# The middle of a decode block's feed-forward as four rows of 448, and w2 with 14 adjacent rows per partition

## Chip, cores, metric

One core of one Trainium2 chip. The metric is the device time of one launch in microseconds. The times are those of repeated runs; the profile is one run of each kernel. All runs told here are in the state that the measurement calls fast.

## The reference

A transformer block for one token: a conditioning vector gives six shifts, scales and gates; grouped-query attention over a cache of 32768 keys; then a feed-forward of width 1792. The part that matters here is the second half:

```python
def _B_ref(x, w1, w2):                       # x [1,1,512], w1 [512,1792], w2 [1792,512]
    h = jnp.einsum('bsd,df->bsf', x, w1)
    h = jnp.maximum(h, jnp.zeros_like(h))
    return jnp.einsum('bsf,fd->bsd', h, w2)
...
h = _layernorm(x, axis=-1) * (1 + cb) + sb
x = x + gb * _B_ref(h, B_w1, B_w2)
```

All weights and the cache are bfloat16. Nearly all of the 149 MB that are read is the cache; w1 and w2 (1.84 MB each) are read last.

## The kernel before

The whole input goes through one DMA queue, in the order in which it is needed: K and V per head group, then wo in four pieces, w1 in two (contraction rows 0 to 2, then row 3 of each partition), w2 in six. The feed-forward before:

```python
FB = 2; FA = FT // FB                                    # FT = 14, FA = 7
w2_v = B_w2.rearrange("(a p b) d -> p a b d", p=P, b=FB) # 2 adjacent rows of w2 per partition and block of 256
W2P = [(0, 2, slice(0, FB)), (2, FA - 5, slice(0, FB)), (FA - 3, 1, slice(0, FB)), (FA - 2, 1, slice(0, FB)),
       (FA - 1, 1, slice(0, 1)), (FA - 1, 1, slice(1, FB))]
...                                                      # second layernorm gives h2T [128, 4], as columns
for part, (k0, k1) in enumerate(W1P):                    # hidden row straight as columns: 4 x 14 matmuls of 1 column
    w1_f = need(("w1", part)).rearrange("p kt (a m b) -> p kt a b m", m=P, b=FB)
    for kt in range(k0, k1):
        for ft in range(FT):
            nc.tensor.matmul(hidT_ps[:, ft:ft + 1], lhsT=w1_f[:, kt - k0, ft // FB, ft % FB, :],
                             rhs=h2T[:, kt:kt + 1], start=False, stop=(kt == KT - 1), ...)
        if kt < KT - 2:
            keep_clock(1)                                # a matmul that nobody reads
nc.scalar.activation(out=<diagonals of hid_bd>, in_=hidT_ps[:].unsqueeze(2).to_broadcast([P, FT, KT]), func=ACT.Relu)
keep_clock(1)
for part, (base, n, bs) in enumerate(W2P):               # 14 x 4 matmuls, output 4 rows of 128
    w2_sb = need(("w2", part))
    ...
                nc.tensor.matmul(ffn_ps, lhsT=hid_bd[:, ft, i, :], rhs=w2_sb[:, a, b - bs.start, i * P:(i + 1) * P], ...)
nc.vector.tensor_tensor(out=o_rows[:], in0=ffn_ps, in1=gb_rows[:], op=ALU.mult)   # the two last VectorE
nc.vector.tensor_tensor(out=o_bf[:], in0=o_rows[:], in1=x1_rows[:], op=ALU.add)   # instructions, then the store
```

## Time and profile before

| | before |
|---|---|
| time, median of the first 3 runs | 355.95 us (355.69 to 356.25) |
| span of the profiled run | 353.6 us |
| HBM read | 149.42 MB, 423 GB/s over the span |
| second layernorm's result h2T starts | 344.52 us |
| last two VectorE instructions start | 350.88 us |

A line of the timeline begins with start and duration in us, then engine, source line, operation, output and input tile, and in brackets how long the engine had stood idle and what ended that. PE is TensorE, PEld its weight loads, DVE VectorE, ACT ScalarE. The lines of this kernel stand in the prediction.

### The profile page before, as it was taken

The numbers are of one execution on the slowest core, as the hardware profiler recorded it, in microseconds if no ns is written. First come the engines' busy times: TensorE is split into PE (matmuls) and PEld (weight loads), VectorE is DVE, ScalarE is ACT, GpSimd is POOL, SyncE is SP. The second block draws the span as 40 slices with busy tenths as digits, with TensorE's granted clock in tenths as the row PEclk, the third lists the DMA queues.
The fourth block names the chain that finished last, engine by engine and source line by source line (L and its number), as shares of the span: only waits on it lengthen the run. The fifth ranks groups of instructions, "written<-read, shape, count | busy, mean of one in ns | idle before, by whom it ended". The sixth has DMA issues, their size and how long they took to land. (4 is left out here: it accounts for less than half of the span.)

```text
span 353.6 us, 4077 instructions
## 1 busy us (share of the span) xinstructions
PE 281.0 (79%) x1351; PEld 113.2 (32%) x1351; DVE 208.0 (59%) x269; ACT 28.2 (8%) x68; POOL 9.7 (3%) x16
## 2 busy tenths in 40 slices
PE   0273781899798979897979796989789787989996
PEld 0031230333243323332433233333333233334445
DVE  7737684982858367572949177553938095743040
ACT  1023004000110011001100101010100010020000
POOL 8200000000000000000000000000000000000000
PEclk9986997699899999998999998799999999999999
DMA  8999999999999999999999999999999999999995
GB/s 309 459 419 430 454 412 423 449 434 419 439 445 419 437 449 417 423 452 426 419 439 445 419 437 442 426 425 445 434 415 441 441 424 423 452 426 413 426 417 197
DMA packets 7108, 149.59 MB, mean 423 GB/s; under 512 B 824, under 2 KB 1080, under 8 KB 2232
## 3 DMA queue, kind: packets, MB, share of 16 engines
q1 hardware_dynamic: 7032, 149.43, 98.5%
q8 instruction: 8, 0.13, 0.1%
q14 instruction: 4, 0.03, 0.0%
q0 software_dynamic: 64, 0.00, 0.0%
HBM read 149.42 MB, written 0.00 MB: 423 GB/s over the span
## 5 line engine op out<-in xcount | busy, mean ns | idle before, releaser
L411 DVE STREAM_TRANSPOSE KTt<-Ksb 128x2048 f32<-128x2048 f32 x64 | 143.3, 2284 | 64.1 <-DMA Ksb<-in_A_k_cache_dram 55.8
L493 PE MATMUL o_ps<-Vsb,PT_g 128*16 (+1 forms) x512 | 129.6, 391 | 21.6 <-ACT qbd L395 9.6
L431 PE MATMUL S_ps<-KTt,qbd 128*128 128x512 bf16 x512 | 122.3, 390 | 18.6 <-DVE KTt L411 17.2
L431 PEld LDWEIGHTS <-qbd 128*128 128x128 bf16 x512 | 49.0, 98 | 83.1 <-issue 25.4
L493 PEld LDWEIGHTS o_ps<-Vsb,PT_g 128*16 x416 | 37.0, 89 | 90.3 <-issue 64.3
L437 DVE TENSOR_SCALAR_CACHE_REDUCE S_g<-S_ps 128x512 f32<-128x512 f32 x16 | 11.0, 690 | 27.6 <-PE S_ps L431 27.6
L395 ACT COPY qbd<-qrep_sb 32x128 bf16<-32x128 bf16 x32 | 9.4, 295 | 135.6 <-PE S_ps L431 134.5
L474 DVE STREAM_TRANSPOSE PT_g<-P_g 128x1024 bf16<-128x1024 bf16 x8 | 9.7, 1218 | 6.6 <-ACT P_g L468 6.6
L465 ACT ACTIVATE nbias<-Mb_ps 128x1 f32<-128x1 f32 x8 | 1.4, 171 | 132.0 <-PE Mb_ps L463 132.0
L233 PE MATMUL xc_ps<-cx_sel,cx_bd 16*128 16x2 bf16 x4 | 0.3, 171 | 14.5 <-DVE cx_bd L227 14.5
L493 PEld LDWEIGHTS <-PT_g 128*16 128x16 bf16 x96 | 8.2, 90 | 11.0
L468 ACT ACTIVATE P_g<-S_g,nbias 128x1024 bf16<-128x1024 f32 x8 | 9.2, 1148 | 0.2
L179 DVE COPY sel<-ident_bf 128x128 bf16<-128x128 bf16 x4 | 8.1, 3936 | 1.1 <-POOL ident_bf masks.py:199 1.1
L524 DVE SCALAR_TENSOR_TENSOR Y<-o_ps,smask,Y 16x128 f32<-16x128 f32 x24 | 8.1, 338 | 0.8
L480 PE MATMUL L_ps<-Lexp,ones_f 128*128 128x4 f32 x16 | 3.0, 257 | 4.3 <-DVE Lexp L477 4.3
L606 PE MATMUL spare_ps<-qbd,ident_bf 128*128 128x512 bf16 x19 | 5.9, 380 | 0.0
L452 DVE TENSOR_REDUCE Mrow<-mT_ps 1x4 f32<-1x128 f32 x8 | 2.1, 257 | 5.9 <-PE mT_ps L449 5.9
L449 PE MATMUL mT_ps<-ident_f,m_p 128*1 128x128 f32 x8 | 2.2, 270 | 3.9 <-DVE m_p L446 2.0
L480 PEld LDWEIGHTS L_ps<-Lexp,ones_f 128*128 128x128 f32 x16 | 3.1, 221 | 5.8 <-issue 5.1
L233 PEld LDWEIGHTS <-cx_bd 16*128 16x128 bf16 x4 | 0.2, 113 | 14.5 <-DVE cx_bd L227 14.5
L543 DVE TENSOR_TENSOR oT_sb<-acc_ps,Linv 128x4 bf16<-128x4 f32 x8 | 1.2, 151 | 5.7 <-PE acc_ps L530 5.7
L368 PE MATMUL q_ps<-wq_sb,hT 128*1 128x512 bf16 x32 | 3.5, 621 | 1.2 <-DVE hT L284 1.2
(114 smaller groups left out, 89.1 us busy)
## 6 DMA issues: line engine op xcount, KB each, us to landing
Ksb<-in_A_k_cache_dram SPq DMA_DIRECT2D x16, 4096.0 KB, 28.2
Vsb<-in_A_v_cache_dram SPq DMA_DIRECT2D x15, 4096.0 KB, 24.6
wq_sb<-in_A_wq_dram SPq DMA_DIRECT2D x1, 4096.0 KB, 19.5
Vsb<-in_A_v_cache_dram SPq DMA_DIRECT2D x2, 2048.0 KB, 23.3
wm_sb<-in_w_mod_dram SPq DMA_DIRECT2D x1, 3072.0 KB, 10.3
wo_sb<-in_A_wo_dram SPq DMA_DIRECT2D x1, 2048.0 KB, 25.0
w_sb<-in_B_w_dram SPq DMA_DIRECT2D x1, 1344.0 KB
wo_sb<-in_A_wo_dram SPq DMA_DIRECT2D x1, 1024.0 KB, 27.1
```

Source lines behind the costliest of these rows:

```text
L179: nc.vector.tensor_copy(out=sel[:, hp, :].rearrange("p (a c) -> p a c", a=4), in_=src)
L368: nc.tensor.matmul(q_ps[i][32 * a:32 * a + 1, :].rearrange("o (h e) -> o h e", e=32), lhsT=hT[:, kt:kt + 1], rhs=wq_f[:, kt, i, a], start= ...
L395: nc.scalar.copy(out=o, in_=i)
L411: t = nc.vector.transpose(out=KTt[:].bitcast(F32), in_=Ksb[:, 32 * half:32 * half + 32, :].rearrange("p j d -> p (j d)").bitcast(F32),)
L431: nc.tensor.matmul(S_ps_tiles[g], lhsT=qbd[g % 2][:, hp, s, :], rhs=KTv[:, 16 * sl:16 * sl + 16, h, :, par], start=(t4 == 0 and sl == 0 an ...
L437: nc.vector.tensor_scalar(out=S_tiles[g][:, G, :], in0=S_ps_tiles[g], scalar1=1.0, scalar2=None, op0=ALU.mult, op1=ALU.max, accum_out=m_ti ...
L468: nc.scalar.activation(out=P_g[:], in_=S_g[:].rearrange("p g f -> p (g f)"), func=ACT.Exp, bias=nbias[:], scale=scale, accum_out=l_g[:],)
L474: nc.vector.transpose(out=PT_g[:], in_=P_g[:])
L480: nc.tensor.matmul(L_ps[:], lhsT=ones_f[:], rhs=Lexp[:], start=True, stop=True)
L493: nc.tensor.matmul(o_tiles[g][:], lhsT=PT, rhs=Vx, start=False, stop=False, skip_group_check=True)
L524: nc.vector.scalar_tensor_tensor(out=Y[:], in0=o[:, s], scalar=smask[:, s:s + 1], in1=Y[:], op0=ALU.mult, op1=ALU.add,)
L606: nc.tensor.matmul(spare[0], lhsT=ident_bf[:], rhs=qbd[0][:, 0, 0:4, :], start=True, stop=True)
```

## The change

Its intent is a shorter way from the second layernorm to w2, and longer runs of memory for w2. The hidden row is computed as rows: h2T is the stationary operand and 448 columns of w1 move past it, four such quarters side by side in the array. VectorE's transpose of 32x32 blocks turns them to columns. Row 448q + 14e + f of the hidden layer then stands at partition 32q + e, so that partition must hold 14 adjacent rows of w2.

```diff
-    W2P = [(0, 2, slice(0, FB)), (2, FA - 5, slice(0, FB)), ...]
+    W2P = [(0, 4), (4, 8), (8, 10), (10, 12), (12, 13), (13, 14)]
-    w2_v = B_w2.rearrange("(a p b) d -> p a b d", p=P, b=FB)
+    w2_v = B_w2.rearrange("(p f) d -> p f d", p=P)
@@ in the attention's tail @@
+        hid_ps = ps_o.tile([P, 512], F32, tag="o", name="hid_ps")
+        nc.vector.memset(hid_ps[:], 0.0)
@@ feed-forward @@
-                for ft in range(FT):
-                    nc.tensor.matmul(hidT_ps[:, ft:ft + 1], lhsT=w1_f[...], rhs=h2T[:, kt:kt + 1], ...)
-                if kt < KT - 2:
-                    keep_clock(1)
+                for q in range(4):
+                    nc.tensor.matmul(hid_ps[32 * q:32 * q + 1, 0:NQ], lhsT=h2T[:, kt:kt + 1],
+                                     rhs=w1_sb[:, kt - k0, q * NQ:(q + 1) * NQ], ...)
+        keep_clock(4)
+        hidT = rows_sb("hidT")...
+        nc.vector.transpose(out=hidT, in_=hid_ps[:, 0:NQ].rearrange("p (e f) -> p f e", f=FT))
         nc.scalar.activation(
-            in_=hidT_ps[:].unsqueeze(2).to_broadcast([P, FT, KT]), func=ACT.Relu,
+            in_=hidT[:, :, 0:1].to_broadcast([P, FT, KT]), func=ACT.Relu,
         )
-        keep_clock(1)
```

(cut; the six pieces keep their sizes, 512, 512, 256, 256, 128 and 128 KB, and the 56 matmuls with w2 stay)

More of the change, by code (lines that the diff above doesn't have):

```diff
@@ L50 @@
     LOOPED = Hkv - 2
-    FB = 2
-    FA = FT // FB
-    W2P = [(0, 2, slice(0, FB)), (2, FA - 5, slice(0, FB)), (FA - 3, 1, slice(0, FB)), (FA - 2, 1, slice(0, FB)),
-           (FA - 1, 1, slice(0, 1)), (FA - 1, 1, slice(1, FB))]
+    W2P = [(0, 4), (4, 8), (8, 10), (10, 12), (12, 13), (13, 14)]
     W1P = [(0, KT - 1), (KT - 1, KT)]
-    assert Dh == 128 and REP == 4 and D == 512 and Dff % (FB * P) == 0 and NTILE == 4
+    assert Dh == 128 and REP == 4 and D == 512 and FT == W2P[-1][1] and NTILE == 4
     scale = float(Dh) ** -0.5
@@ L125, in load @@
         else:
-            a0, n, bs = W2P[key[1]]
-            nb = bs.stop - bs.start
-            t = piece("w12_sb", KT * Dff + (a0 * FB + bs.start) * D, n * nb * D)
-            t = t.rearrange("p (a b d) -> p a b d", a=n, b=nb)
-            src = w2_v[:, a0:a0 + n, bs]
+            f0, f1 = W2P[key[1]]
+            t = piece("w12_sb", KT * Dff + f0 * D, (f1 - f0) * D).rearrange("p (f d) -> p f d", d=D)
+            src = w2_v[:, f0:f1]
         stream_dma(t[:], src)
@@ L693 @@
         project(3)
-        hidT_ps = small_ps([P, FT], "hidT_ps")
-        nc.vector.memset(hidT_ps[:], 0.0)
         stat2 = const.tile([P, 2], F32)
@@ L716 @@
         nc.vector.tensor_copy(out=x1_rows[:], in_=x1_ps[0])
+        NQ = 32 * FT
         for part, (k0, k1) in enumerate(W1P):
-            w1_f = need(("w1", part)).rearrange("p kt (a m b) -> p kt a b m", m=P, b=FB)
+            w1_sb = need(("w1", part))
             for kt in range(k0, k1):
-                for ft in range(FT):
+                for q in range(4):
                     nc.tensor.matmul(
-                        hidT_ps[:, ft:ft + 1], lhsT=w1_f[:, kt - k0, ft // FB, ft % FB, :], rhs=h2T[:, kt:kt + 1],
-                        start=False, stop=(kt == KT - 1), skip_group_check=True,
-                    )
-                if kt < KT - 2:
-                    keep_clock(1)
+                        hid_ps[32 * q:32 * q + 1, 0:NQ], lhsT=h2T[:, kt:kt + 1],
+                        rhs=w1_sb[:, kt - k0, q * NQ:(q + 1) * NQ], start=False, stop=(kt == KT - 1),
+                        skip_group_check=True,
+                    )
+        keep_clock(4)
+        hidT = rows_sb("hidT").rearrange("p a b -> p (a b)")[:, 0:NQ].rearrange("p (f e) -> p f e", e=32)
+        nc.vector.transpose(out=hidT, in_=hid_ps[:, 0:NQ].rearrange("p (e f) -> p f e", f=FT))
         hb = hid_bd[:]
@@ L729 @@
             out=AP(hb.tensor, hb.offset, [hb.ap[0], [KT * KT, FT], [KT + 1, KT]]),
-            in_=hidT_ps[:].unsqueeze(2).to_broadcast([P, FT, KT]), func=ACT.Relu,
+            in_=hidT[:, :, 0:1].to_broadcast([P, FT, KT]), func=ACT.Relu,
         )
-        keep_clock(1)
         ffn_ps = bank("ffn_ps")[0:KT, 0:P]
-        last = len(W2P) - 1
-        for part, (base, n, bs) in enumerate(W2P):
+        for part, (f0, f1) in enumerate(W2P):
             w2_sb = need(("w2", part))
-            for a in range(n):
-                for b in range(bs.start, bs.stop):
-                    ft = (base + a) * FB + b
-                    for i in range(KT):
-                        nc.tensor.matmul(
-                            ffn_ps, lhsT=hid_bd[:, ft, i, :], rhs=w2_sb[:, a, b - bs.start, i * P:(i + 1) * P],
-                            start=(part == 0 and a == 0 and b == 0 and i == 0), stop=(ft == FT - 1 and i == KT - 1),
-                        )
+            for ft in range(f0, f1):
+                for i in range(KT):
+                    nc.tensor.matmul(
+                        ffn_ps, lhsT=hid_bd[:, ft, i, :], rhs=w2_sb[:, ft - f0, i * P:(i + 1) * P],
+                        start=(ft == 0 and i == 0), stop=(ft == FT - 1 and i == KT - 1),
+                    )
         o_rows = const.tile([KT, P], F32)
```

## The prediction

> **What bounds the kernel now.** I read four views in this order: the page (bytes, chain of work that ended last), the timeline of the last ten microseconds, the DMA queue's own timeline in slices (for the landings), and the instructions of the few lines that the change resembles.
>
> The page first.
>
> ```profile
> span 353.6 us, 4077 instructions
> PE 281.0 (79%) x1351; PEld 113.2 (32%) x1351; DVE 208.0 (59%) x269; ACT 28.2 (8%) x68; POOL 9.7 (3%) x16
> DMA  8999999999999999999999999999999999999995
> HBM read 149.42 MB, written 0.00 MB: 423 GB/s over the span
> DMA Vsb<-in_A_v_cache_dram 7%; DMA w_sb<-in_B_w_dram 5%; PE ffn_ps L742 1%; SPq L139 0%; DVE o_rows L747 0%; DVE o_bf L749 0%
> ```
>
> The row of DMA digits is at 9 from the second slice to the last but one: 149 MB are streamed once, and no engine is as full. The chain ends in two transfers, 40 matmuls and two small VectorE instructions. The change does not touch one byte of the total, so it can only act in the tail, behind the last weight transfers. The chain in order of time gives the tail:
>
> ```profile
> 331.74 16.67 DMA w_sb<-in_B_w_dram
> 348.45 2.41 PE ffn_ps L742 x40
> 350.88 0.29 DVE o_rows L747
> 351.19 0.28 DVE o_bf L749
> ```
>
> The piece of w2 that was issued at 331.74 landed at about 348.41. It is the second of six, and the 40 matmuls after it are those of pieces 2 to 6 (10 rows per partition, 4 matmuls each). The timeline shows what lies ahead of them:
>
> ```profile
> 344.52 0.22 DVE L284 SCALAR_TENSOR_TENSOR h2T<-cen_ln,rstd_ln,modT_sb 128x4 bf16<-128x4 f32 x1
> 344.77 0.42 PEld L721 LDWEIGHTS <-w_sb 128*128 128x128 bf16 x14 [0.46 <-DMA w_sb<-in_B_w_dram]
> 345.93 0.84 PE L721 MATMUL hidT_ps<-h2T,w_sb 128*128 128x1 bf16 x28
> 346.86 0.29 ACT L728 ACTIVATE hid_bd<-hidT_ps 128x56 bf16<-128x56 f32 x1 [2.58 <-PE hidT_ps L721]
> 347.24 1.05 PE L742 MATMUL ffn_ps<-w_sb,hid_bd 128*4 128x128 bf16 x16 [0.23 <-ACT hid_bd L728]
> 348.45 2.39 PE L742 MATMUL ffn_ps<-w_sb,hid_bd 128*4 128x128 bf16 x40 [0.16 <-DMA w_sb<-in_B_w_dram]
> ```
>
> Read the brackets: the last line waits for a DMA, not for the hidden row. The 16 matmuls of piece 1 end at 347.24 + 1.05 = 348.29 and then TensorE has nothing until 348.45.
>
> Landings, as issue plus time to landing of each transfer (from the DMA view in narrow windows): w1 rows 0 to 2 at 344.75 (where the issuing engine's wait for that transfer also ends), w1 row 3 at 322.42 + 23.4 = 345.82; w2 pieces 1 to 6 at 326.86 + 20.2 = 347.06, 331.74 + 16.7 = 348.42, 336.59 + 12.5 = 349.09, 339.03 + 10.7 = 349.73, 340.28 + 9.7 = 349.98 and 341.55 + 8.8 = 350.35. So the whole tail runs at the pace at which bytes arrive. The 40 matmuls are 39 gaps of (2.39 - 0.219)/39 = 0.0557 us and a last one of 0.219 us. Without any wait all 56 from 347.24 would end at 347.24 + 55 x 0.0557 + 0.219 = 350.52, against 350.84 in the trace: 0.32 us of slack on the side that computes the hidden row. And the last piece, landing at 350.35, needs 4 matmuls, 3 x 0.0557 + 0.219 = 0.39: 350.74 at the earliest. Two floors made of transfers, 350.84 and 350.74, lie close together.
>
> **What the Trainium skill says.** "TensorE: Matmul & The Clock Gate", section "Part 3: Packing small matmuls — row/col tiling": outputs at PSUM partitions 0, 32, 64 and 96 sit in separate column groups of the array, and their matmuls run together. The trace agrees: the 16 matmuls of one output row and 512 columns for the attention projection took 1.08 us, 67 ns each, where one alone shows 378 ns. "VectorE: DVE Perf Modes", section "The three transpose paths": VectorE transposes 32x32 blocks only. That is why each quarter of the hidden row is put at a partition that is a multiple of 32, and why partition 32q+e must then own 14 adjacent rows of w2. "DMA: Bandwidth & Descriptors", section "Why small descriptors are slow (HBM only)": a fixed overhead of about 3 cycles per packet, named for 256-byte ones. The trace leans the same way at larger sizes: 432 GB/s from 20 to 320 us with a mean packet of 29 KB, 400 and 388 GB/s in 345.82 to 347.06 and 347.06 to 348.44, with DMA share at 1.04 and 1.03. "TensorEngine Tiling (Array Packing)", section "Tiling Modes": changing the mode drains the array. No line isolates that cost; the mode is changed twice here, where TensorE waits anyway.
>
> **The change part by part.**
>
> Removed: 56 one-column matmuls for the hidden row (rows 0 to 2 with two clock-keeping matmuls between, 344.80 to about 346.3, row 3 to 346.77) and the 0.07 us memset of their 14 columns.
>
> Added on TensorE: 16 matmuls of one row by 448 columns. A round of four took, in the like group, (1.08 - 0.378)/15 x 4 = 0.187 us at 512 columns; I take 0.19 for 448. Rows 0 to 2 start at 344.80 as now and are through their issue at 344.80 + 3 x 0.19 = 345.37. Then row 3 of w1 isn't there: it lands at 345.82. Here the old order was never kept waiting, since it got to row 3 only at about 346.3; the new one is. From 345.85 the last round takes 3 x 0.047 + 0.35 (one matmul, 0.378 less the shorter row) = 0.49 at most; the four overlap nearly wholly, so 0.36 to 0.49, and I take 0.40: 346.25.
>
> Added on VectorE: the transpose of 128x448 float32 out of PSUM, read with a stride. The like instruction, 128x512 with a stride of 4, took 0.705 us, the contiguous one 0.696: the stride costs nearly nothing. Less 64 elements at 0.97 per ns (the long transposes: 2048 in 2284 ns, 512 in about 700, so 1536 in 1584 ns), 0.066: 0.64 us. Start 0.04 after the matmuls (the gap between 350.84 and 350.88): 346.29 to 346.93.
>
> Moved on ScalarE: the relu now reads SBUF with a stride of 32. It took 294 ns on 56 columns; the cast of 16 columns from a strided SBUF tile took 216. I keep 0.28: 346.97 to 347.25. First matmul of w2 at about 347.33, against 347.24. The path through the hidden row is therefore no shorter: 0.52 us gained at the end of the matmuls (346.77 to 346.25), 0.64 + 0.04 paid for the transpose, a little back on the relu; about 0.1 us later. That fits in the slack of 0.32: 56 matmuls from 347.33 end at 350.61.
>
> Four clock-keeping matmuls, 0.213 us apart, begin after the 16 and end by about 347.1, before the relu: nothing.
>
> The new memset of 128x512 takes 0.485 us of VectorE at about 333.5, where VectorE is idle for over 3 us: nothing. The order of instructions, compared engine by engine, is otherwise unchanged, and the issues of the eight weight transfers have the same sizes and waits.
>
> Transfers: pieces 1 and 2 of w2, 512 KB each, become runs of 4 KB instead of 2 KB; pieces 3 and 4 stay at 2 KB, 5 and 6 at 1 KB. Row 3 of w1 is already made of 3.5 KB runs at the pitch that w2 gets (14336 bytes): 448 KB between 344.75 and 345.82, 429 GB/s between the landings, against 1048576 B in 2.60 us = 403 GB/s for the two pieces. At 429 they take 2.44: up to 0.16 us earlier for everything behind. The windows put less difference on it (381 GB/s in row 3's stretch), so I take 0.08.
>
> Sum: piece 2 lands at 348.34, end of matmuls 348.34 + 0.03 + 2.39 = 350.76; last piece at 350.27, 350.27 + 0.03 + 0.39 = 350.69; hidden-row path 350.61. The latest counts: 350.76 against 350.84, so 0.08 us earlier; the two VectorE instructions and the store stay. 355.95 - 0.08 = 355.87 us.
>
> **The rivals.**
>
> 1. The transpose path becomes the bound. It would need the relu to end over 0.25 us later than I have it: a strided PSUM read at half speed adds 0.47 us to the transpose and 0.2 to 0.3 us to the time, 356.2. The like transpose with stride 4 speaks against it; a stride of 14 has no line here.
> 2. The transfers gain the full 0.16 us or more and the hidden path stays in its slack: 355.75. For it, the 429 GB/s; against it, the last two 1 KB pieces, where the rate falls to 221 GB/s and less whatever comes before.
> 3. The scattered runs (4 KB out of every 14 KB, instead of a solid 256 KB block) cost the transfers 5%: 2.60 us becomes 2.73, 356.05. Row 3 of w1, with the same pitch, speaks against it.
> 4. TensorE drops its clock in the wait from 345.37 to 345.82. The granted clock is 1.00 in all of the last 24 us, and the gap is too short beside gaps already there (0.23). At half speed 56 matmuls would take 3 us more, 358 us. Unlikely.
>
> **Range and chances.** All but the last rival lie within 0.3 us. The three runs of before span 0.56 us (355.69 to 356.25), more than any of it, and the profiled run was 355.37; so the range is set by the scatter: 355.3 to 356.4. Two per cent are 7.1 us, and the whole stretch from the second layernorm to the end is 9.0 us (342.49 to 351.47), so most of it would have to vanish: faster 0.01, within 2% 0.98, slower 0.01.
>
> **What would show it right or wrong.** In the new trace: 12 matmuls of 448 columns, then a wait of about 0.4 us that a weight transfer ends; a transpose of 0.64 us; a relu of under 0.3 us ending at about 347.25; the 40 last matmuls still ahead of a DMA wait, or no wait at all before the first 20; landings of pieces 2 and 6 0 to 0.16 us earlier. A transpose over 0.9 us or a granted clock below 1 would speak for rivals 1 or 4; later landings at equal rates up to 345 us for rival 3. A difference that arises before 344 us would mean that something I hold untouched was moved.

## The result, and the profile after

The changed kernel took 355.41 us, median of 6 runs (355.13 to 355.82); the kernel before took 355.82 us in its 6 runs (355.47 to 356.27). A ratio is the mean time of one kernel's fast runs over that of the other's fast runs of the same rounds, so not quite the ratio of the medians: 0.9988, with a 95% interval of 0.9975 to 1.0001. That is "same" at two per cent, and the interval just touches 1.

The timeline of the changed kernel, from the layernorm's result to the last VectorE pair:

```profile
344.33 0.22 DVE L278 SCALAR_TENSOR_TENSOR h2T<-cen_ln,rstd_ln,modT_sb 128x4 bf16<-128x4 f32 x1
344.67 0.74 PE L717 MATMUL hid_ps<-w_sb,h2T 128*1 128x448 bf16 x12
345.66 0.36 PE L717 MATMUL hid_ps<-w_sb,h2T 128*1 128x448 bf16 x4 [0.25 <-DMA w_sb<-in_B_w_dram]
346.07 0.65 DVE L724 STREAM_TRANSPOSE hidT<-hid_ps 128x448 f32<-128x448 f32 x1 [1.32 <-PE hid_ps L717]
346.82 0.33 ACT L726 ACTIVATE hid_bd<-hidT 128x56 bf16<-128x56 f32 x1 [2.71 <-DVE hidT L724]
347.19 3.37 PE L736 MATMUL ffn_ps<-w_sb,hid_bd 128*4 128x128 bf16 x56 [0.20 <-ACT hid_bd L726]
350.61 0.28 DVE L741 TENSOR_TENSOR o_rows<-ffn_ps,gb_rows 4x128 f32<-4x128 f32 x1 [3.88 <-PE ffn_ps L736]
```

Twelve matmuls run, then TensorE waits for row 3 of w1, as foretold. The whole tail here lies 0.19 us earlier than in the profile of before already at h2T. This is the prediction's own sign that something untouched was moved ("a difference that arises before 344 us"), but it comes from the stream of transfers, which varies from run to run: its last packet of 32 KB ended at 321.46 us here and at 321.66 before, ahead of the first changed instruction (the memset at 333.50), and in the other profiles below at 321.5 to 322.1. From the start of h2T to the start of the last VectorE pair it is 350.61 - 344.33 = 6.28 us, against 350.88 - 344.52 = 6.36 before: 0.08 us less, the number predicted.

The 56 matmuls stand in one line because no idle time shows between them, but 3.37 us is 0.09 more than the 55 x 0.0557 + 0.219 = 3.28 that they need without a wait. A matmul shows 0.219 us and the next starts 0.056 after it, so a wait of under 0.16 us can't be seen as idle time. The landing of piece 2 (the end of its transfer, as its semaphore tells) says where it is: issued at 331.56, landed at 348.13, while matmul 17 was ready at 347.19 + 16 x 0.0557 = 348.08. With the 0.04 us from landing to first matmul that the kernel before shows (348.41 to 348.45) this is the 0.09. So both floors, the hidden row and piece 2, now lie within 0.1 us of each other.

The packets changed as the diff says. Times below are computed from the packets of the two traces (medians; the size is the run of memory):

```
bytes    before: count, ns    after: count, ns    bytes per ns
 4096          256   159           512   159         25.8
 2048          768    84           256    84         24.4
 1024          256    46           256    46         22.3
32768         4096  1213          4096  1213         27.0
```

A packet costs some 9 ns and 1 ns per 27.2 bytes. Pieces 1 and 2 are 256 packets fewer, 16 per transfer engine, so 16 x 9 = 0.14 us of transfer by this estimate. Piece 2 landed at 348.41 before (331.74 + 16.67; the prediction's "331.74 + 16.7 = 348.42" doesn't add up, but its result is only 0.01 off) and at 348.13 after: 0.28 us earlier, less some 0.2 of the whole stream.

The traces hold the landings to the nanosecond, and with row 3 of w1 as the mark the stream's own scatter drops out. From the landing of row 3 to that of piece 2, the five profiles with w2 as before (before, e1, e1b, e7, e7b) have 2.57 to 2.63 us; the eight with the new layout (changed kernel twice, e2, e4, e8, e8b, e9, e11) have 2.51 to 2.56. The means are 2.616 and 2.537: the longer runs bring piece 2 forward by 0.08 us, about half of the estimate.

### The profile page after: what moved, and what is told of

Read it like the earlier page. It is cut to its first block, busy times and chain, and to the rows that moved or that the text cites. A ratio compares the mean times of both kernels' runs of the same rounds, so it can differ in the third digit from the quotient of the medians.

```text
span 353.3 us, 3999 instructions
## 1 busy us (share of the span) xinstructions
PE 282.0 (80%) x1310; PEld 112.9 (32%) x1312; DVE 209.1 (59%) x270; ACT 28.3 (8%) x68; POOL 9.7 (3%) x16
## 5 line engine op out<-in xcount | busy, mean ns | idle before, releaser
L425 PE MATMUL S_ps<-KTt,qbd 128*128 128x512 bf16 x512 | 124.6, 396 | 17.0 <-DVE KTt L405 15.6
L295 PE MATMUL mod_ps<-wm_sb,siluT 128*1 128x512 bf16 x24 | 3.6, 624 | 1.1 <-DVE siluT L289 1.1
```

Of the source, the lines that this page charges most:

```text
L295: nc.tensor.matmul(dst[j // 4][32 * (j % 4):32 * (j % 4) + 1, :], lhsT=src_T[:, kt:kt + 1], rhs=w[:, kt, j * 512:(j + 1) * 512], start=(kt ...
L425: nc.tensor.matmul(S_ps_tiles[g], lhsT=qbd[g % 2][:, hp, s, :], rhs=KTv[:, 16 * sl:16 * sl + 16, h, :, par], start=(t4 == 0 and sl == 0 an ...
```

## The experiments

Theory A, that of the prediction: landings set the end, the longer runs of w2 bring piece 2 forward, and the hidden row's path stays in its slack. Rival B: the new way from h2T to the relu brings the gain. Rival C: the transfers have room, the runs' size is indifferent. Theory D came after the first four runs and is told there. The edits are shown shortened.

### Four rows and transpose alone, w2 as before: e1_rows_only, e1b_rows_only

```diff
+    W2P, w2_v, load and the last 56 matmuls as in the kernel before
-                        rhs=w1_sb[:, kt - k0, q * NQ:(q + 1) * NQ], ...
+                        rhs=w1_sb[:, kt - k0, :].rearrange("p (a q x) -> p a q x", q=4, x=64)[:, :, q, :], ...
-        nc.vector.transpose(out=hidT, in_=hid_ps[:, 0:NQ].rearrange("p (e f) -> p f e", f=FT))
+        nc.vector.transpose(out=hidT.rearrange("p (a b) e -> p a b e", b=FB),
+                            in_=hid_ps[:, 0:NQ].rearrange("p (a e b) -> p a b e", a=FA, b=FB))
```

> The four rows and the transpose alone, with w2 as before (pieces of 2 adjacent rows per partition, runs of 2 KB). Theory A (the end is set by landings, the new runs of 4 KB bring piece 2 some 0.1 us forward, the hidden row stays inside its slack): piece 2 lands as in the kernel before, TensorE waits for it, and from the end of the second layernorm (h2T) to the first of the two last VectorE instructions it takes 6.36 us as before, not 6.28 as in the changed kernel; the time is that of before within 0.2 us. Rival B (the faster matmuls of the hidden row bring the gain): 6.28 us, as in the changed kernel, and no wait before matmul 17 of the last 56.

The first version gave a wrong result (relative error 0.053): I had put the axes of the transpose's input in the order a, e, b. Its times are still of use, since the same instructions run on other values, but for the order in which the transpose reads: 355.35 us median of 5 runs (before, in those rounds, 355.96). The profile: h2T at 344.51, last VectorE pair at 350.90, so 6.39 us, as in the kernel before and not 6.28; piece 2 landed at 348.43. That is theory A's number, and rival B's is not met. But the time is not theory A's: it was to be that of before within 0.2 us, and the median is 0.61 lower, though this kernel lacks the long runs. The version with the axes right:

> As e1_rows_only, with the transpose's axes put right: the four rows and the transpose with w2 as before. Theory A (landings set the end in most runs, the 4 KB runs bring piece 2 forward): landings of the kernel before, a wait for piece 2 inside the last 56 matmuls, 6.36 to 6.39 us from h2T to the last VectorE pair, against 6.28 in the changed kernel. Theory D, formed after the first four runs (there are two kinds of tail: in some runs TensorE loses about 1.2 us around 296 to 303 us at a granted clock near 0.75, h2T is then done at 345.7 instead of 344.5 and the computation, not the landings, sets the end; there the new way from h2T to the relu is some 0.3 us shorter): this kernel gains in late runs alone, so its times scatter less than those of before, and its median is 0 to 0.5 us lower.

355.42 us median of 5 runs (355.19 to 355.69), before 355.64 (355.33 to 356.56), ratio 0.9990 (0.9976 to 1.0005); correct. Its profile fell into another kind of run:

```profile
345.13 0.22 DVE L283 SCALAR_TENSOR_TENSOR h2T<-cen_ln,rstd_ln,modT_sb 128x4 bf16<-128x4 f32 x1
345.41 0.93 PE L722 MATMUL hid_ps<-w_sb,h2T 128*1 128x448 bf16 x16
350.93 0.28 DVE L753 TENSOR_TENSOR o_rows<-ffn_ps,gb_rows 4x128 f32<-4x128 f32 x1 [3.88 <-PE ffn_ps L748]
```

h2T comes 0.6 us later than in the first version's profile, yet the end is the same: 5.80 us between them. The expectation of 6.36 to 6.39 therefore missed: there was no wait for row 3 of w1, since it had landed (at 345.83) before TensorE wanted it. The wait for piece 2 was there, but small: the 56 matmuls took 3.38 us, 0.09 more than without a wait.

### w2 in the new layout alone: e2_layout_only

```diff
+    hidden row as 56 one-column matmuls, as in the kernel before, with
+            w1_f = need(("w1", part)).rearrange("p kt (m f) -> p kt f m", m=P)
```

> w2 as 14 adjacent rows per partition in the new pieces, but the hidden row still as 56 one-column matmuls, whose weights are now read from w1 with a stride of 14 elements instead of 2. Theory A: landings as in the changed kernel (pieces 1 and 2 in 128 packets of 4 KB, some 0.1 us earlier against the stream), 6.25 to 6.3 us from h2T to the last VectorE pair. If the stride of 14 slows the weight loads from 96 ns to over 150, the hidden row comes later by 56 x 0.03 or more and ends the chain instead: over 6.6 us. Rival B: no gain over before, 6.36 or more, even at the same weight loads.

359.13 us (before 355.96): 3.2 us slower. The group of its hidden-row weight loads and matmuls (count, shortest, median and longest ns), and the same of the kernel before:

```profile
L716 PEld LDWEIGHTS <-w_sb x56: 137/158/160, 345.6 to 349.6; 128*128 128x128 bf16 x56
L716 PE MATMUL hidT_ps<-h2T,w_sb x56: 163/198/200, 346.0 to 349.6; 128*128 128x1 bf16 x56
```

```profile
L721 PEld LDWEIGHTS <-w_sb x56: 96/96/97, 344.8 to 346.6; 128*128 128x128 bf16 x56
L721 PE MATMUL hidT_ps<-h2T,w_sb x56: 163/163/165, 344.8 to 346.6; 128*128 128x1 bf16 x56
```

A weight load that reads every fourteenth element took 158 ns instead of 96, at a granted clock of 1.00 (the share of its full clock that TensorE was allowed, as the profile records it). From h2T to the first matmul with w2 this run has 350.26 - 345.71 = 4.55 us, against 2.72 before. Not all of the 3.2 us is due to that: the granted clock fell to 0.55 from 350 to 352 us as well, and the last 56 matmuls took 4.87 us instead of 3.28. The two parts of the change belong together: the layout of w2 alone makes the columns dear, and rows avoid that. Piece 2 landed 2.54 us after row 3 of w1, as in the changed kernel, so the layout alone does bring the landing forward; only the hidden row is too late here to use it.

### All runs of w2 at 512 bytes: e3_512_byte_runs

```diff
-            t = piece(...)                            # destination without gaps
+            t = piece(...).rearrange("p (a x) -> p a x", x=D // 2 + 16)[:, :, 0:D // 2]
```

> The changed kernel with all of w2 written into SBUF with a gap after every 256 elements, so that every run is 512 bytes instead of 4, 2 and 1 KB. The packets of the tail took 159 ns at 4 KB, 84 at 2 KB, 46 at 1 KB, which is 9 ns and 27.2 bytes per ns; so 28 ns at 512 bytes. Per transfer engine 16 x 159 + 16 x 84 + 16 x 46 = 4.62 us become 224 x 28 = 6.27. Theory A: the last landing 1.65 us later and the end 1.3 to 1.8 us later than in the changed kernel, piece 2 some 1.0 us later. Rival C (the transfers of w2 have room behind the computation, the size of their runs is indifferent): within 0.3 us of the changed kernel.

356.40 us (356.33 to 356.60), 1.0 us above the changed kernel's 355.41 (of other rounds) and 0.44 above the kernel before in the same rounds (ratio 1.0016, 1.0003 to 1.0030). The last 56 matmuls:

```profile
347.62 1.05 PE L738 MATMUL ffn_ps<-w_sb,hid_bd 128*4 128x128 bf16 x16 [0.40 <-DMA w_sb<-in_B_w_dram]
349.32 2.58 PE L738 MATMUL ffn_ps<-w_sb,hid_bd 128*4 128x128 bf16 x40 [0.65 <-DMA w_sb<-in_B_w_dram]
351.93 0.28 DVE L743 TENSOR_TENSOR o_rows<-ffn_ps,gb_rows 4x128 f32<-4x128 f32 x1 [4.99 <-PE ffn_ps L738]
```

Two waits for transfers that no other engine explains: rival C is out, the landings of w2 reach the end. A packet took 27 ns (28 expected). The size was off, 1.0 us instead of 1.3 to 1.8, since the expectation took the last landing to move by the whole 1.65 us; counted from row 3 of w1, it moved by 1.16. The transfer engines had not all been busy to the end (in the kernel before, their mean share is 0.62 from 348 to 350 us), and that spare time can take up a part; this wasn't tested by itself. The issuing queue also changed: one of its issues of w2 lasted 11.0 us, and the last piece was issued at 347.4 instead of 341.35. So for pieces 3 to 6 the cost of the packets and the late issue can't be told apart; piece 2, issued in time at 331.71, took 17.6 us to land instead of 16.6, where some 1.0 more was expected. Here the runs were also nearly equal to each other, a first sign that a floor of transfers hides what varies elsewhere.

### The transpose twice: e4_two_transposes

```diff
+        nc.vector.transpose(out=hidT0, in_=hid_ps[:, 0:NQ].rearrange("p (e f) -> p f e", f=FT))
         nc.vector.transpose(out=hidT, in_=hid_ps[:, 0:NQ].rearrange("p (e f) -> p f e", f=FT))
```

> The changed kernel with the transpose of the hidden row done twice, one after the other: 0.65 us more on the path from the hidden row to the relu. Theory A: in the changed kernel the hidden row and the landing of piece 2 are within 0.1 us of each other, so nearly all of it shows: the 56 last matmuls run without a wait and end 0.55 to 0.7 us later than in the changed kernel, 6.85 to 6.95 us from h2T to the last VectorE pair. Rival C2 (the landings alone set the end and the hidden row has 0.3 us of room, as it had before): 0.3 to 0.4 us later.

356.00 us (355.61 to 356.53), 0.6 us above the changed kernel's first set and 0.4 above its second (355.61, below). From h2T to the last VectorE pair the profile has 352.03 - 345.79 = 6.24 us, not 6.85 to 6.95. But h2T itself started at 345.79 here, 1.46 us later than in the profile of the changed kernel, long before anything that this experiment touches, so the expected 6.85 to 6.95, made for the other kind of run, was missed. Against the changed kernel's second profile, with h2T at 345.73 and 5.71 us, it is 0.53 us more, and by just that much the last transpose ends later after h2T (348.23 - 345.79 = 2.44 us against 347.64 - 345.73 = 1.91). So the path through the transpose does carry to the end, in runs of this kind wholly.

### What makes the two kinds of run: theory D

The runs with a late h2T have something in common long before. The busy time of each engine in two stretches (columns: stretch, its length, then busy us and count of PE, PEld, DVE, ACT and POOL, the granted TensorE clock, DMA share, GB/s), first the kernel before, then a second profile of the changed kernel, unaltered:

```profile
290.00:296.00 6.00, 3.79 (x18) 1.87 (x19) 5.72 (x13) 1.41 (x3) 0.00 (x0) 1.00 1.01 434
296.00:304.00 8.00, 7.12 (x32) 2.69 (x30) 2.30 (x6) 0.00 (x0) 0.00 (x0) 1.00 0.97 418
```

```profile
290.00:296.00 6.00, 3.70 (x16) 1.78 (x17) 5.72 (x13) 1.41 (x3) 0.00 (x0) 0.94 1.00 429
296.00:304.00 8.00, 7.34 (x24) 2.89 (x23) 2.24 (x6) 0.00 (x0) 0.00 (x0) 0.62 0.96 414
```

In the second, TensorE was granted 0.62 of its clock from 296 to 304 us and got through 24 matmuls where the first got through 32. In the profiles that can be compared from h2T to the end:

| profile | clock 296 to 304 us | h2T starts | last VectorE pair | between |
|---|---|---|---|---|
| before | 1.00 | 344.52 | 350.88 | 6.36 |
| changed | 1.00 | 344.33 | 350.61 | 6.28 |
| e1_rows_only | 1.00 | 344.51 | 350.90 | 6.39 |
| e1b_rows_only | 0.85 | 345.13 | 350.93 | 5.80 |
| changed, second (e10) | 0.62 | 345.73 | 351.44 | 5.71 |
| e4 (transpose twice) | 0.58 | 345.79 | 352.03 | 6.24 |

The others fit: e3 with 1.00 and h2T at 344.46, e2 with 0.60 and 345.71, and of the version below with four column groups one profile with 0.62 and 345.48, one with 1.00 and 344.37. By and large, the lower the clock there, the later h2T; the transfers of w2 land at nearly the same times (piece 2 of w2 at 348.48 in the changed kernel's second profile). The early profiles have such a dip too, only elsewhere: the clock is 0.50 from 218.0 to 224.7 us in the kernel before and from 256.7 to 263.4 in the changed one, against 295.4 to 302.0 in its second profile. So it is the place of the dip that goes with a late h2T. That it causes it is not shown by an experiment, for no run moved the dip on purpose. The tail of the late one:

```profile
345.73 0.22 DVE L278 SCALAR_TENSOR_TENSOR h2T<-cen_ln,rstd_ln,modT_sb 128x4 bf16<-128x4 f32 x1
346.01 0.93 PE L717 MATMUL hid_ps<-w_sb,h2T 128*1 128x448 bf16 x16
348.11 3.29 PE L736 MATMUL ffn_ps<-w_sb,hid_bd 128*4 128x128 bf16 x56 [0.21 <-ACT hid_bd L726]
```

Sixteen matmuls run without a wait, and then 56 without a wait. So in early runs the landings set the end, and in late ones the computation does. Theory D: in late runs the new way is shorter than the old one, by an amount that an early profile can't show.

No profile of the kernel before fell into a late run, so I made late runs of both kernels.

### Both kernels made late: e7_before_late, e8_after_late, then e7b and e8b

```diff
         nc.vector.tensor_tensor(out=x1T[:], in0=attnT_ps, ...)
+        late = rows_sb("late")
+        for _ in range(3):
+            nc.vector.memset(late[:, 0, :], 0.0)
```

> The kernel before, with three idle fills of a 128x512 tile put on VectorE between the first two steps of the second layernorm, so that h2T comes 0.9 to 1.5 us later in every run and the landings of w2 no longer matter. Theory D: all 56 last matmuls run without a wait; from h2T's start to the last VectorE pair some 0.22 + 2.41 + 0.09 + 3.28 + 0.04 = 6.05 us.

> The changed kernel with the same three fills. Theory D: no wait for row 3 of w1 among the 16 matmuls, h2T to the last VectorE pair 0.22 + 2.1 + 0.05 + 3.3 + 0.04 = 5.7 us, 0.2 to 0.45 us less than e7_before_late, and its time lower than that kernel's by the same. Theory A alone, in which the change acts only through the landings: no difference between the two.

358.72 us (356.57 to 360.87) and 357.90 us (356.36 to 359.02): the sign is as expected, but it says little, since the experiment was spoiled. In both profiles the clock fell for the tail itself, in the second one to 0.54 from 346 to 348 us, in the first one so:

```profile
342.00:344.00 2.00, 1.09 (x17) 0.55 (x16) 1.13 (x3) 0.00 (x0) 0.00 (x0) 1.00 0.93 384
344.00:346.00 2.00, 1.17 (x6) 0.43 (x6) 1.47 (x10) 0.29 (x1) 0.00 (x0) 0.92 1.03 398
346.00:348.00 2.00, 2.00 (x27) 1.08 (x27) 0.57 (x3) 0.00 (x1) 0.00 (x0) 0.50 1.05 402
```

TensorE had stood idle beside the fills, once for 1.67 us, and ran at 0.50 from 346 us on. The second try put six more of the kernel's own clock-keeping matmuls beside the fills:

```diff
-        keep_clock(3)
+        keep_clock(9)
```

> As e7_before_late, with 6 more clock-keeping matmuls beside the three fills, since there TensorE stood idle for 1.7 us and its granted clock fell to 0.50 for the whole tail, which spoiled the comparison. Theory D: granted clock 1.00 to the end, h2T some 1.8 us later than in the kernel before, all 56 last matmuls without a wait, 6.05 us from h2T to the last VectorE pair; time 356.8 to 357.6.

> The changed kernel with the same fills and the same 6 matmuls. Theory D: 5.7 to 5.8 us from h2T to the last VectorE pair, 0.25 to 0.35 us less than e7b_before_late; time 0.1 to 0.6 us lower than that kernel's. Theory A alone (the change acts through the landings only): equal.

356.85 us (356.76 to 357.09) against 356.36 us (356.29 to 356.61): every run of the second is faster than every run of the first, by 0.49 us in the medians. Both were run on the same chip in the same rounds. The timelines, old way first:

```profile
346.58 0.22 DVE L284 SCALAR_TENSOR_TENSOR h2T<-cen_ln,rstd_ln,modT_sb 128x4 bf16<-128x4 f32 x1
348.93 0.29 ACT L731 ACTIVATE hid_bd<-hidT_ps 128x56 bf16<-128x56 f32 x1 [2.58 <-PE hidT_ps L724]
349.28 3.29 PE L745 MATMUL ffn_ps<-w_sb,hid_bd 128*4 128x128 bf16 x56 [0.21 <-ACT hid_bd L731]
352.60 0.28 DVE L750 TENSOR_TENSOR o_rows<-ffn_ps,gb_rows 4x128 f32<-4x128 f32 x1 [5.61 <-PE ffn_ps L745]
```

```profile
346.21 0.22 DVE L278 SCALAR_TENSOR_TENSOR h2T<-cen_ln,rstd_ln,modT_sb 128x4 bf16<-128x4 f32 x1
346.49 0.93 PE L720 MATMUL hid_ps<-w_sb,h2T 128*1 128x448 bf16 x16
347.47 0.65 DVE L727 STREAM_TRANSPOSE hidT<-hid_ps 128x448 f32<-128x448 f32 x1 [0.84 <-PE hid_ps L720]
348.59 3.29 PE L739 MATMUL ffn_ps<-w_sb,hid_bd 128*4 128x128 bf16 x56 [0.20 <-ACT hid_bd L729]
351.91 0.28 DVE L744 TENSOR_TENSOR o_rows<-ffn_ps,gb_rows 4x128 f32<-4x128 f32 x1 [3.80 <-PE ffn_ps L739]
```

From h2T to the first matmul with w2 it is 349.28 - 346.58 = 2.70 us by the old way and 348.59 - 346.21 = 2.38 by the new one: 0.32 us less. From h2T to the last VectorE pair, 6.02 against 5.70: the same 0.32. The changed kernel's own late profile has 5.71, as e8b; the 6.02 of the old way is shown by the kernel made late alone. Theory D's numbers (6.05, and 0.25 to 0.35 less) hold, and theory A alone, which has the two equal, doesn't. The 0.17 us that the medians show beyond 0.32 I can't place; the two profiles differ by 0.37 us already at h2T, and by 0.39 at the landing of row 3 of w1, so that part is the stream's.

### The changed kernel again, and a version with four column groups: e10_after_again, e9_groups, e11_groups_again

> The changed kernel once more, unaltered, for a second set of times on a chip and a second profile. If its granted clock dips between 296 and 304 us, h2T starts at 345.4 to 345.8 and the end of the last matmuls follows 5.7 us after it, with no wait for row 3 of w1 and none for piece 2; otherwise h2T at 344.3 to 344.6 and the wait for row 3 as before. Time 0 to 0.5 us under the kernel before.

355.61 us (355.32 to 355.93) against 355.96 (355.39 to 356.50), ratio 0.9990 (0.9977 to 1.0004): the first result again. The profile is the late one of the table: 5.71 us, 16 matmuls without a wait, as expected.

The last version tries to beat both. If late runs are bound by 56 matmuls in a row, the first 40 can share the array in four column groups, and be added at the end:

```diff
-                        ffn_ps, lhsT=hid_bd[:, ft, i, :], ...
+                        part_ps[32 * (ft % 4):32 * (ft % 4) + KT, 0:P] if ft < 10 else ffn_ps, lhsT=hid_bd[:, ft, i, :], ...
+            if f1 == 10: nc.vector.tensor_copy(out=part_sb[:], in_=part_ps[:, 0:P])
+            if f1 == 13: nc.tensor.matmul(ffn_ps, lhsT=place32[:, 0:KT], rhs=part_sb[:], start=False, ...)
```

> A version meant to beat both: the changed kernel, in which the first 10 of the 14 rows of w2 go to four column groups of the array (partitions 0, 32, 64, 96 of a separate bank), are copied to SBUF while the last 4 rows run as now, and are added by one more matmul before the last piece. If the four groups overlap, 40 matmuls take some 1.2 to 1.5 us instead of 2.3. By the landings (theory A) it ends where the last piece allows, 0.05 to 0.15 us before the changed kernel in early runs; in late runs (theory D) 0.5 to 0.8 us before it. Median 0.1 to 0.5 us under the changed kernel. If the groups don't overlap (56 ns each as now) it is equal or up to 0.3 us slower.

> The version with four column groups once more, beside the changed kernel on the same chip. Its end depends less on h2T, so its times should scatter less: 355.3 to 355.6; median 0 to 0.3 us under e10_after_again.

355.44 us in both sets (355.31 to 355.59 and 355.28 to 355.75; before 355.64 and 355.96; ratios 0.9991 and 0.9989, both intervals reaching over 1). Beside the changed kernel on the same chip it is 0.17 us lower in the median, 355.44 against 355.61, with ranges that overlap; the runs were to stay within 355.3 to 355.6 and reached 355.75. Sixteen matmuls took 0.43 us instead of 1.05, so the groups do overlap. The second profile (h2T at 344.37, an early run) shows the price:

```profile
348.23 0.43 PE L740 MATMUL part_ps<-w_sb,hid_bd 128*4 128x128 bf16 x16 [0.55 <-DMA w_sb<-in_B_w_dram]
349.50 0.83 PE L740 MATMUL ffn_ps<-w_sb,hid_bd 128*4 128x128 bf16 x12 [0.23 <-DMA w_sb<-in_B_w_dram]
350.17 0.38 PE L749 MATMUL ffn_ps<-part_sb,place 128*4 128x128 f32 x2
350.81 0.28 DVE L753 TENSOR_TENSOR o_rows<-ffn_ps,gb_rows 4x128 f32<-4x128 f32 x1 [1.19 <-PE ffn_ps L740]
```

TensorE waits for piece after piece, and the added matmul stands ahead of the last four: the pair starts at 350.81, 0.20 us later than in the changed kernel's early profile, where the expectation had 0.05 to 0.15 earlier. In the late run of the first set (h2T at 345.48) the pair started at 350.82, 5.34 us after h2T and 0.37 less than the changed kernel's 5.71 (0.62 earlier by the clock of the profile, as the expected 0.5 to 0.8, but 0.25 of that is an earlier h2T). So it evens the two kinds of run out, and is no clear gain over the changed kernel.

## Why the prediction was right or wrong

- **Total and class.** Predicted 355.87 with a range of 355.3 to 356.4, measured 355.41 and, in the second set, 355.61. Right, but in a range as wide as the scatter. The change itself was put at 0.08 us; the medians differ by 0.41 and 0.35, four to five times as much, though not clear of the scatter.
- **What bounds the kernel.** Right for early runs: landings of w1's row 3 and w2's piece 2 end the waits, and runs of 512 bytes moved the end by 1.0 us.
- **Sizes of the parts.** The transpose took 0.65 us (0.64), the last round of four matmuls 0.36 (0.40), the relu 0.33 (0.28); the wait for row 3 was there, 0.25 us of idle TensorE (about 0.4). The four matmuls of a round overlap, as foretold: 16 took 0.93 us in e8b_after_late, where one alone shows 0.35. No run isolates the cost of changing the array's mode, or tests the limit of 32x32 blocks. Rivals 1, 3 and 4 are out for the early profile: a stride of 14 did not slow the transpose, the longer runs landed earlier and not later, and the clock stayed at 1.00 from 344 us on. From h2T to the first matmul with w2 2.86 us (347.19 - 344.33) against 2.72 before, so 0.14 later where 0.1 was predicted. Piece 2 landed 0.08 us earlier against row 3 (0.08, chosen between 0 and 0.16). The tail came out 0.08 us shorter, the predicted sum; an agreement to that digit is luck, since the hidden row, predicted to keep 0.15 us of room, came within 0.1 us of piece 2, and two profiles that should agree differ by 0.03 us (6.36 before, 6.39 in e1_rows_only).
- **The step that failed** is "the path through the hidden row is therefore no shorter". It holds only where TensorE must wait for row 3 of w1. Where h2T is late, that wait is gone and the new way is 0.32 us shorter (2.38 us against 2.70 in e8b and e7b). The prediction read the path from one profile, an early one, and took its place of h2T for that of every run.
- **"The range is set by the scatter"** was right as a range and wrong as a reading: I took the spread of 0.56 us among the runs of before as noise without a cause. In the profiles, h2T's place goes with the granted clock at 296 to 304 us, and that place decides which floor ends the kernel. Rival 4, the loss of the clock, was looked for only in the last 24 us.
- **What stays open.** How often runs are late is not known, since only profiled runs show h2T, and no late profile of the unaltered kernel before was taken. (The changed kernel's two profiled runs took 355.13 us, early, and 355.93, late: just the lowest and the highest of its 11 times, so the two kinds may well be most of its spread.) So how the mean gain of 0.3 to 0.4 us divides between the 0.08 us of early runs and the 0.32 us of late ones is argued, not shown. The gain itself is not clear of scatter (both intervals of the changed kernel reach 1). That e1b_rows_only, without the long runs, has nearly the ratio of the changed kernel (0.9990 against 0.9988 and 0.9990) suggests that most of it comes from the shorter way; it isn't proof at these intervals.

## What to carry to other kernels

Where a tail waits for its last transfers, list the landing of each piece and the computation's own time, and take the latest: a change that shortens only one of them is worth the distance to the next. Before calling a spread between runs noise, compare a mark such as the start of the last stage across several profiles, with the granted clock ahead of it: a shorter path may pay only in the runs that come late. And give a delay experiment its own clock-keeping work, or it measures the clock.

## What the Trainium skill lacked or had wrong

- "DMA: Bandwidth & Descriptors", section "Specifications", gives 512 bytes as the least transfer for line rate. Here a 512-byte packet took 27 ns, 19 bytes per ns, against 27.0 at 32 KB: 70%. The packets of 1, 2 and 4 KB reached 22.3, 24.4 and 25.8.
- "TensorE: Matmul & The Clock Gate", section "Why this matters for your kernels", warns of idle gaps over about 3 us. A shorter one was enough here: in e7_before_late the longest idle time of TensorE in the 7 us before the clock fell to 0.50 was 1.67 us, in a stretch of 4 us in which it was busy for 1.09 + 1.17 us; with six more matmuls there (e7b_before_late) the clock stayed at 1.00.
- The same page, section "LDWEIGHTS (loading the stationary operand)", has the weight load depend on the number of columns alone. With the columns 14 elements apart instead of 2 the load of 128 columns took 158 ns instead of 96, at a clock of 1.00. The skill isn't silent on spacing, though: another of its pages, "SBUF — State Buffer", section "Door 1: The DMA port swizzle", says that accesses which cross to a new 16-byte line pay for it. What is missing is the word of it here, and the size.
